# An expert stage with its turns in another order, two turns in plain float32, and gate scatters in the second stage

## The chip, the cores and the metric

One core of one Trainium2 chip runs the kernel. The metric is the device time of one launch in microseconds; the time of a kernel is the median of its runs.

## The reference

Three stages follow each other: attention within clusters, a mixture of eight experts with one expert per token, and a bilinear layer.

```python
def _attn_ref(q, k, v, centroids):            # 2 x 8 heads, 768 rows, 64 wide; 16 centroids
    ...
    mask = q_assign[:, :, :, None] == k_assign[:, :, None, :]
    scores = np.where(mask, scale * np.matmul(q, k.transpose(0, 1, 3, 2)), -1000000000.0)
    ...
    return np.matmul(attn, v)

def _moe_ref(x, expert_emb, tau, w1, w2):     # 1536 tokens of 512; 8 experts, 1024 hidden features
    ...
    expert_idx = np.argmax(logits, axis=1)
    gate_w = probs[np.arange(N), expert_idx]
    for e in range(E):
        mask = expert_idx == e
        h = np.maximum(x[mask] @ w1[e], 0.0)
        out[mask] = gate_w[mask, None] * (h @ w2[e])
    return out

def _moe2_ref(x, w_a, w_b, w_out):            # 512 -> 1536 -> 512
    return ((x @ w_a) * (x @ w_b) @ w_out)
```

The weights `w_a`, `w_b` and `w_out` of the last layer arrive as 64-bit numbers, all else as float32.

## The kernel before

The order of the work on every engine is the order in which the program is written; nothing reorders it. The program runs attention first (to 299.6 us of the trace), then a loop over `G`: 64 steps of the **expert stage** and 72 steps of the **second stage**, which is the bilinear layer.

**Turns.** The expert stage takes the experts in eight turns of eight steps. Turn 0 is expert 0; `ranks` sorts the others by their token counts on the chip and writes the order into `turn_i`, which SyncE and ScalarE read into registers for the addresses of their loads. `WIDTHS` gives the token columns of each turn; before, they fall from 256 to 160 in the order of the turns. `limits` works out which tokens exceed the widths, `further` where each turn's results go, and `rare` is a block for the excess tokens that is jumped over here (at step `GR` = 5, on every engine that has a part in it).

**A step.** `layer1(G)` makes 128 hidden features of a turn into a PSUM tile (`et0`, `et1` in alternation), ScalarE applies the relu, and `layer2(G - 2)` adds the product with `w2` to the turn's results `ys_ps` in the PSUM banks `sc0` to `sc3`. `trans_x` turns the next turn's tokens at step 5 of a turn (6 in turn 0), and `load_xe` loads them on ScalarE's queue.

**Two halves.** To keep float32 precision with the faster `float32r` format, every operand is split into a rounded high half and the rest as a low half. Three products (high by high, low by high, high by low) make one result. Turns 0 to 2 (`e < TWO`) issue them as three matmuls; later turns issue two, of which the first takes both halves of the tokens side by side (columns twice the width) into two PSUM halves that VectorE adds (`both_halves`, L1162) before it makes the low half of the hidden features (L1157).

**Weights.** An expert has 4 chunks of weights, and each chunk 4 parts of 128 rows by 512. `load_raw` (L151) loads two parts (512 KB) into one of `NRAW` = 4 raw buffers, on SyncE's queue; `split_some` makes the high half on ScalarE (L177) and the low half on VectorE or, for one pair in four from turn 3 on, on GpSimd (L178). The split halves lie in `NSLOT` = 9 chunk slots. A limit (`2 * G + lead`, and a ramp until step 22) sets how far the splits run ahead. After the last split, `narrow_a` to `narrow_d` do the same for the 64-bit weights of the second stage, one part in a step: ScalarE (L1015, L1035) and VectorE (L1027, L1028, L1029, L1041).

**Routing tables.** `result_rows` (turn 2) and `gates` (from step 25 on) work out where a token's row lies and its gate. `gates` then issues twelve scatters of 128 pairs into `tab_d` on GpSimd (L909), each followed by a one-element copy from a tile of the current step (L915), and the read of the table into `res` on SyncE (L917). `res` is needed when the second stage stores its first results. `put_rows` writes a turn's results to `ys_d` on SyncE, and `load_x2` reads columns of `ys_d` for the second stage.

**Second stage.** `bil1(I)` makes 128 columns of both products with 24 matmuls, VectorE multiplies them (L1242), and `bil2(I - 2)` multiplies with `w_out` into the banks `sc0` to `sc3`, `pp` and `pv`.

Of the kernel before, what the change touches and what calls it, by code (L numbers as in the profile page):

```python
# [9 lines left out]
F32 = mybir.dt.float32  # L10
F32R = mybir.dt.float32r
# [13 lines left out]
CAP = 256  # L25
WIDTHS = (256, 256, 248, 224, 216, 192, 176, 160)
TWO = 3
NRAW = 4
# [5 lines left out]
PACE = (1,)  # L34
YW = 0
CG0 = 2
# [8 lines left out]
def kernel(  # L45
# [76 lines left out]

    units = [(m, 2) for m in range(0, 4 * NCE, 2)]
    units += [(m, 1 if wide else 2) for m in range(4 * NCE, 4 * NCH, 1 if wide else 2)]
# [10 lines left out]
    def load_raw():  # L135
        u = nraw[0]
        if u == len(units) or (u >= NRAW and sum(units[u - NRAW]) > ndone[0]):
            return
        m, cnt = units[u]
        if 16 <= m < 4 * NCE and m % 16 == 0:  # L140
            if not ranked:
                return
            turn_e[m // 16] = nc.values_load(turn_i[0:1, m // 16:m // 16 + 1], engines=[mybir.EngineType.SP], min_val=1, max_val=NE - 1)
        nraw[0] += 1
        src = streamed(m // 4)[:, m % 4:m % 4 + cnt, :]
        if src.dtype == I64:
            t = rawp.tile([P, cnt, 512, 2], I32, tag="raw", name=f"raw_{u}")
            nc.sync.dma_start(out=t.rearrange("p c f x -> p c (f x)"), in_=src.bitcast(I32))
        else:
            t = rawp.tile([P, cnt, 512], F32, tag="raw", name=f"raw_{u}")  # L150
            nc.sync.dma_start(out=t, in_=src)  # L151
        for j in range(cnt):
            raw[m + j] = t[:, j]
        if cnt == 2:
            raw2[m] = t

    def open_part():
        n, j = divmod(nsplit[0], 4)  # L160
        if j == 0:

            hl[n] = (big if n % NSLOT else left).tile([P, 2, 4, 512], F32R, tag=f"w{n % NSLOT}", name=f"w_{n}")
        w = raw.pop(nsplit[0])
        nsplit[0] += 1
        return w, hl[n][:, 0, j, :], hl[n][:, 1, j, :]

    def split_some(m):

        for _ in range(m // 2):  # L170
            load_raw()
# [138 lines left out]
    def setup_rest():  # L310
# [581 lines left out]

    def gates(hh):

# [63 lines left out]
    def ranks():  # L958
# [4 lines left out]
        nc.vector.tensor_reduce(out=pbase.rearrange("p o e -> p (o e)"), in_=bef, axis=AX.X, op=ALU.add)  # L963
        nc.vector.tensor_tensor(out=at, in0=row(turn_c), in1=col(pbase), op=ALU.is_equal)
        nc.vector.tensor_tensor(out=prod[0:1], in0=at[0:1].rearrange("p e q -> p q e"), in1=turn_c[0:1].to_broadcast([1, NE, NE]), op=ALU.mult)
# [13 lines left out]
    def further():  # L979

        nc.vector.tensor_tensor(out=prod, in0=col(turn_c), in1=row(turn_c), op=ALU.is_gt)
        summed(obase, prod, row(over))
        summed(pbase, bef, row(held))
        nc.vector.tensor_reduce(out=key[:, 0, 0:1], in_=over.rearrange("p o e -> p (o e)"), axis=AX.X, op=ALU.add)
# [70 lines left out]
    def trans_x(key, src):  # L1055

        x = new_x(key)
# [5 lines left out]
        wd = WIDTHS[key]  # L1063
        for u in range(2):
# [71 lines left out]
    def layer1(G):  # L1136
# [4 lines left out]
        wd = WIDTHS[e]  # L1141
        h2 = big.tile([P, 2, CAP], F32R, tag="hh", name=f"hh_{G}", bufs=4)
# [3 lines left out]
        if e < TWO:  # L1146
            mm3(ph[:, 0, :wd], [(ws[j], (x[:, 0, j, :wd], x[:, 1, j, :wd])) for j in range(DC)])
# [15 lines left out]

    ready = []

    def layer2(G):
# [3 lines left out]
        h2 = hs.pop(G)  # L1170
        wd = WIDTHS[e]
        hh, hlo = h2[:, 0, :wd], h2[:, 1, :wd]
        last = f == NF - 1
        if f == 0:
            banks = (2, 3, 0, 1) if e >= TWO else (e % 2 * 2, e % 2 * 2 + 1)
            ys_ps[e] = [ps_s.tile([P, 2, CAP], F32, tag=f"sc{u}", name=f"y_{e}_{u}") for u in banks]
        if e < TWO:
            for i, (s_, m_) in enumerate(((hh, 0), (hh, 1), (hlo, 0))):
                for j in range(DC):
                    nc.tensor.matmul(ys_ps[e][j // 2][:, j % 2, :wd], w[:, m_, ff, j * P:(j + 1) * P], s_,  # L1180
                                     start=(f == 0 and i == 0 and j % 2 == 0), stop=(last and i == 2 and j % 2 == 1))
        else:
# [185 lines left out]
```

## Time and profile before

| what | value |
|---|---|
| median of 3 runs (lowest, highest) | 802.11 us (799.87, 802.85) |
| profiled execution | 805.78 us, its span 803.4 us |
| TensorE matmul busy | 767.8 us, 96% of the span |
| VectorE busy | 494.9 us, 62% |
| ScalarE busy | 402.3 us, 50% |
| GpSimd busy | 128.2 us, 16% |
| first matmul of the expert stage | 299.64 us |
| first matmul of the second stage | 487.10 us |

The shares are means over three stages with different limits. What bounds the expert stage is read from TensorE's idle time and granted clock in stretches of that stage, from what ended each idle time, and from the instructions that the named engine ran just before.

### The profile page before, as it was taken

What the parts mean: (1) busy time and instruction counts of PE and PEld (TensorE: products, weight loads), DVE (VectorE), ACT (ScalarE), POOL (GpSimd) and SP (SyncE); (2) the same over time, 40 slices, a digit from 0 to 9 for tenths busy, and PEclk for the clock granted to TensorE, in tenths of its full rate; (3) what the DMA queues carried; (4) which work ended last, traced back from release to release, by engine and by line L of the source; (5) the groups of instructions that cost most, each with busy time, mean ns of one, the idle gap of its engine ahead of it and who ended that gap; (6) DMA issues with size and microseconds to landing.
All of it is one profiled execution on the core that took longest, in us unless ns stands there. A gap on an engine that the chain in (4) does not pass through costs nothing.

```text
span 803.4 us, 14115 instructions
## 1 busy us (share of the span) xinstructions
PE 767.8 (96%) x5385; PEld 669.4 (83%) x5385; DVE 494.9 (62%) x998; ACT 402.3 (50%) x860; POOL 128.2 (16%) x145
## 2 busy tenths in 40 slices
PE   8899999998999988998999888999999999999996
PEld 5667777776777668997999877999999999999996
DVE  6677676785657666787888799777762322221221
ACT  4556766767666674575676655444432222221211
POOL 5103203043100050012228500000001110000101
PEclk9899999999999999999999989999999999999999
DMA  6228123163121035788779867534401200000000
GB/s 187 52 75 281 40 79 83 56 190 95 44 46 31 32 126 188 237 283 274 254 250 227 219 222 228 156 115 128 132 1 53 78 28 1 2 27 1 27 1 26
DMA packets 48970, 91.95 MB, mean 114 GB/s; under 512 B 6264, under 2 KB 22264, under 8 KB 48896
## 3 DMA queue, kind: packets, MB, share of 16 engines
q1 hardware_dynamic: 44688, 81.01, 33.8%
q0 software_dynamic: 2304, 6.31, 2.1%
q10 hardware_dynamic: 1904, 3.67, 1.3%
q8 instruction: 43, 0.70, 0.4%
q14 instruction: 31, 0.25, 0.1%
HBM read 69.27 MB, written 14.04 MB: 104 GB/s over the span
## 4 chain that ended last, share of the span: by engine, by line
issue 42%; DMA 7%; PE 6%; POOL 2%; DVE 2%; ACT 1%; POOLq 0%; DVEq 0%; ACTq 0%; SPq 0%
DMA raw<-in_moe_w_dram 6%; PE h L1152 2%; PE y L1184 2%; DVE w L178 1%; ACT w L177 1%; POOL out_dram L1280 1%; POOL w L178 1%; PE h L1153 1%; PE y L1185 1%; DMA tab_d<-id_gate,slot_i 1%; PE y L1180 0%; DMA res<-tab_d 0%; PE h L1075 0%; DVE rr L878 0%; POOL tab_d L909 0%
## 5 line engine op out<-in xcount | busy, mean ns | idle before, releaser
L1075 PEld LDWEIGHTS ab<-xT_b,w 128*128 128x128 f32 x1152 | 143.8, 191 | 5.8 <-DVE hf L1162 2.1
L1075 PE MATMUL ab<-xT_b,w 128*128 128x256 f32 x1152 | 145.4, 282 | 1.9 <-DVE hf L1162 1.9
L1242 DVE TENSOR_TENSOR ga<-ab,ga 128x256 f32<-128x256 f32 x72 | 30.5, 424 | 150.3 <-ACT ga L1241 150.3
L533 ACT ACTIVATE E<-sc,nmx 128x768 f32<-128x768 f32 x96 | 86.8, 905 | 58.9 <-DVE nmx L528 47.7
L1241 ACT COPY ga<-ab 128x256 f32<-128x256 f32 x72 | 26.9, 373 | 172.3 <-PE ab L1075 172.3
L1269 PE MATMUL o<-w,g 128*128 128x512 f32 x432 | 111.4, 394 | 1.6 <-DVE ys L1162 1.6
L528 DVE TENSOR_REDUCE nmx<-sc 128x1 f32<-128x768 f32 x96 | 91.4, 953 | 17.9 <-PE sc L520 16.2
L548 PEld LDWEIGHTS et<-ident,E 128*128 128x128 f32 x576 | 64.0, 143 | 37.8 <-ACT ET L552 12.4
L548 PE MATMUL et<-ident,E 128*128 128x128 f32 x576 | 84.2, 283 | 7.0 <-ACT E L533 3.2
L1269 PEld LDWEIGHTS o<-w,g 128*128 128x128 f32 x432 | 76.7, 189 | 14.6 <-DVE ys L1162 1.8
L554 DVE COPY ET<-et 128x384 f32<-128x384 f32 x96 | 52.6, 548 | 57.4 <-PE et L548 57.3
L177 ACT CAST w<-raw 128x1024 fp32r<-128x1024 f32 x64 | 67.4, 1055 | 31.7 <-DMA raw<-in_moe_w_dram 26.4
L178 DVE TENSOR_TENSOR w<-raw,w 128x1024 fp32r<-128x1024 f32 x54 | 65.5, 1217 | 16.6 <-ACT w L177 16.2
L575 PE MATMUL pv<-ET,v 128*64 128x384 f32 (+2 forms) x408 | 74.2, 485 | 0.6 <-ACT ET L552 0.5
L519 PE MATMUL sc<-K,Q 80*128 80x512 f32 x192 | 73.3, 382 | 0.0
L1280 POOL DMA_INDIRECT out_dram<-ot,res x12 | 11.7, 972 | 330.8 <-DVE ot L1279 329.5
L520 PE MATMUL sc<-K,Q 128*128 128x512 f32 x192 | 62.0, 344 | 0.0
L1152 PE MATMUL h<-xT,w 128*128 128x448 f32 (+4 forms) x160 | 51.0, 373 | 4.7 <-DVE hf L1162 2.6
L1184 PE MATMUL y<-hh,w 128*128 128x448 f32 (+4 forms) x160 | 50.9, 373 | 3.5 <-DVE ys L1162 3.5
L1075 PE MATMUL ab<-x2h,w 128*128 128x256 f32 x384 | 53.6, 282 | 0.0
L1075 PEld LDWEIGHTS ab<-x2h,w 128*128 128x128 f32 x384 | 50.8, 191 | 2.0
L1245 ACT CAST g<-ga 128x256 fp32r<-128x256 f32 x72 | 29.3, 406 | 39.1 <-DVE ga L1242 39.1
(254 smaller groups left out, 1349.3 us busy)
## 6 DMA issues: line engine op xcount, KB each, us to landing
raw<-in_moe_w_dram SPq DMA_DIRECT2D x64, 512.0 KB, 5.2
raw<-in_moe_w_a_dram SPq DMA_DIRECT2D x12, 512.0 KB, 3.5
raw<-in_moe_w_b_dram SPq DMA_DIRECT2D x12, 512.0 KB, 3.8
raw<-in_moe_w_out_dram SPq DMA_DIRECT2D x12, 512.0 KB, 3.5
xs_d<-zero SPq DMA_DIRECT2D x8, 512.0 KB, 6.2
xe<-xs_d ACTq DMA_DIRECT2D x7, 512.0 KB, 5.7
v<-in_v_dram SPq DMA_DIRECT2D x8, 384.0 KB, 3.1
K<-K SPq DMA_DIRECT2D x8, 384.0 KB, 3.9
```

Source lines behind the costliest of these rows:

```text
L177: nc.scalar.copy(hi, w)
L178: (nc.gpsimd if n >= 4 * TWO and n % 2 == 0 and j == 0 else nc.vector).tensor_sub(lo, w, hi)
L519: nc.tensor.matmul(ps[:, lo:hi], Q3[:, qs], K3[:, h * S + lo:h * S + hi], start=True, stop=False)
L520: nc.tensor.matmul(ps[:, lo:hi], Q2[:, qs], K2[:, h * S + lo:h * S + hi], start=False, stop=True)
L528: nc.vector.tensor_reduce(out=nmx[pp][:, h, t:t + 1], in_=sc[s], axis=AX.X, op=ALU.max, negate=True)
L533: nc.scalar.activation(e, sc.pop(s), AF.Exp, bias=nmx[pp][:, h, t:t + 1], accum_out=sums[pp][:, t, h:h + 1])
L548: nc.tensor.transpose(pt[:, j * P:(j + 1) * P], e[:, kt * P:(kt + 1) * P], ident)
L575: nc.tensor.matmul(pv[h * D:(h + 1) * D, :], vt[:, h, kt, :], ets[g, h][:, kt, :n * P], start=(kt == 0), stop=(kt == NT - 1))
L1075: nc.tensor.matmul(ps, s_, m_, start=(i == 0), stop=(i == len(ops) - 1))
L1152: nc.tensor.matmul(ph[:, :, :wd], ws[j][0], x[:, :, j, :wd], start=(j == 0), stop=False)
L1184: nc.tensor.matmul(ys_ps[e][j][:, :, :wd], w[:, 0, ff, j * P:(j + 1) * P], h2[:, :, :wd], start=(f == 0), stop=False)
L1269: nc.tensor.matmul(o_ps[ck][t], s_[:, t * P:(t + 1) * P], w_[:, m_], start=(f == 0 and i == 0), stop=(f == NF2 - 1 and j == len(o_f[ck]) - ...
```

## The change

- `WIDTHS` becomes 256, 160, 256, 224, 248, 216, 192, 176: turn 1 is now the narrowest, turn 7 the second narrowest. `RANKS` gives each turn's place in the sorted order, and `further` works out the turn order of the result rows from it (three more instructions on VectorE).
- `KINDS`: turns 0, 2 and 4 issue three matmuls, turns 3, 5 and 6 two, and turns 1 and 7 ("one") a single matmul in plain float32, with no low halves: of their weights, of their tokens and of their hidden features. Their results need two PSUM banks and one copy each on ScalarE and VectorE.
- The weights of turns 1 and 7 are loaded straight into their chunk slots (`load_whole`), past the raw buffers, with no split. The loads of turn 1 stand at steps 3 and 5, those of turn 7 at steps 42, 46 and 50. `skip_whole` lets the splits go on with the next turn.
- All remaining splits have their low half on VectorE.
- `ranks` and `limits` move from ahead of the loop to steps 1 and 2, `further` from step 6 to step 8, and the first `load_xe` from step 1 to 2. `put_rows` writes one step later (`YW`).
- `gates` keeps its arithmetic; its scatters and the read of `res` become `put_gates`, one scatter in each of the second stage's first twelve steps.
- The PSUM banks of a turn's results are taken in the order in which they came free (`y_banks`).

```diff
-WIDTHS = (256, 256, 248, 224, 216, 192, 176, 160)
-TWO = 3
+WIDTHS = (256, 160, 256, 224, 248, 216, 192, 176)
+RANKS = (0, 7, 1, 3, 2, 4, 5, 6)
+KINDS = ["three" if w > 224 else "two" if w > 176 else "one" for w in WIDTHS]
...
-YW = 0
+YW = 1
...
+    wholes = [4 * n + j for n in whole for j in (0, 2)]
+
+    def load_whole(G):
+
+        while wholes and wholes[0] < min(4 * (NSLOT + 2 * (max(G - LAG, 0) // 4)), 2 * G + 40, 4 * NCE if G >= GR else 4 * (NSLOT - 3)):
+            n, j = divmod(wholes.pop(0), 4)
+            if j == 0:
+                if n % 4 == 0:
+                    take_turn(n // 4)
+                slot(n, F32)
+            nc.sync.dma_start(out=hl[n][:, 0, j:j + 2, :], in_=streamed(n)[:, j:j + 2, :])
+
+    def skip_whole():
+        while nsplit[0] // 4 in whole:
+            nsplit[0] += 4
+            ndone[0] += 4
...
-            (nc.gpsimd if n >= 4 * TWO and n % 2 == 0 and j == 0 else nc.vector).tensor_sub(lo, w, hi)
+            nc.vector.tensor_sub(lo, w, hi)
...
+        summed(turn_of, at, row(turn_c))
+        nc.vector.tensor_tensor(out=bef, in0=col(turn_of), in1=row(turn_of), op=ALU.is_gt)
...
-    ranks()
-    limits()
...
+        if kind == "one":
+            for j in range(DC):
+                nc.tensor.matmul(ph[:, 0, :wd], ws[j][0], x[:, 0, j, :wd], start=(j == 0), stop=(j == DC - 1))
+            nc.scalar.activation(hh, ph[:, 0, :wd], AF.Relu)
+        elif kind == "three":
...
-            banks = (2, 3, 0, 1) if e >= TWO else (e % 2 * 2, e % 2 * 2 + 1)
+            y_banks.sort(key=lambda u: y_free[u])
+            take = y_banks[:4 if kind == "two" else 2]
...
+        if G == 1:
+            ranks()
+        if G == 2:
+            limits()
...
         elif I < tot:
             bil1(I)
+            next(pg_, None)
...
+        if 3 <= G < total_f:
+            load_whole(G)
```

Three places show the order on an engine before and now.

VectorE, at the head of the expert stage, before: the end of `limits`, then the first low half of weights (`w`) of the loop and the low half of the hidden features of step 0 (`hh`).

```order
L975 TENSOR_TENSOR held<-cnt,cap 128x8
L976 TENSOR_TENSOR over<-cnt,held 128x8
L977 TENSOR_REDUCE most<-over 1x1
L178 TENSOR_TENSOR w_3518<-raw_2153,w_3518 128x1024
L1149 SCALAR_TENSOR_TENSOR hh_3523<-h_3524,hh_3523 128x256
```

The same place now:

```order
L968 TENSOR_TENSOR cnt<-cnt_p,ebase 128x8
L205 TENSOR_TENSOR w_3515<-raw_2162,w_3515 128x1024
L1192 SCALAR_TENSOR_TENSOR hh_3520<-h_3521,hh_3520 128x256
L205 TENSOR_TENSOR w_3515<-raw_2239,w_3515 128x1024
L994 SCALAR_TENSOR_TENSOR key<-cnt,iota_e 128x8
L995 MEMSET key 128x1
L996 TENSOR_TENSOR bef<-key 128x64
```

Two low halves of weights and the hidden features of step 0 now stand ahead of `ranks` (from `key` on), which came ahead of them.

VectorE in turn 7, one step, before: the sum and low half of the hidden features, then one part of a 64-bit weight (three instructions on `a`, then the low half of the part before it).

```order
L1162 TENSOR_TENSOR hf_7090<-h_7081,hf_7090 128x160
L1157 SCALAR_TENSOR_TENSOR hh_7080<-hf_7090,hh_7080 128x160
L1027 TENSOR_SCALAR a_7076<-a_7076 128x512
L1028 SCALAR_TENSOR_TENSOR a_7076<-raw_6927,a_7076 128x512
L1029 SCALAR_TENSOR_TENSOR a_7076<-raw_6927,a_7076 128x512
L1041 TENSOR_TENSOR w_7021<-a_7022,w_7021 128x512
```

Two steps of turn 7 now:

```order
L1060 TENSOR_SCALAR a_6945<-a_6945 128x512
L1061 SCALAR_TENSOR_TENSOR a_6945<-raw_6822,a_6945 128x512
L1062 SCALAR_TENSOR_TENSOR a_6945<-raw_6822,a_6945 128x512
L1074 TENSOR_TENSOR w_6911<-a_6912,w_6911 128x512
L1060 TENSOR_SCALAR a_6965<-a_6965 128x512
L1061 SCALAR_TENSOR_TENSOR a_6965<-raw_6854,a_6965 128x512
L1062 SCALAR_TENSOR_TENSOR a_6965<-raw_6854,a_6965 128x512
L1074 TENSOR_TENSOR w_6911<-a_6945,w_6911 128x512
```

The two instructions on the hidden features are gone; the weights of the second stage stay.

TensorE in turn 7, before: the end of one `layer2` and the head of the next `layer1`.

```order
L1184 MATMUL y_1_7098<-hh_7116,w_6704 128x2x160
L1185 MATMUL y_1_7098<-hh_7116,w_6704 128x160
L1152 MATMUL h_7218<-xT_6899,w_6783 128x2x160
L1153 MATMUL h_7218<-xT_6899,w_6783 128x160
L1152 MATMUL h_7218<-xT_6899,w_6783 128x2x160
```

One whole step of turn 7 now:

```order
L1187 MATMUL h_6950<-xT_6761,w_6410 128x176 x4
L1230 MATMUL y_0_6923<-hh_6880,w_6545 128x176 x2
L1230 MATMUL y_1_6924<-hh_6880,w_6545 128x176 x2
L1187 MATMUL h_6970<-xT_6761,w_6548 128x176 x4
L1230 MATMUL y_0_6923<-hh_6916,w_6545 128x176 x2
```

A step of turn 1 or 7 has 8 float32 matmuls, where a step of turns 6 and 7 had 16 in pairs.

## Rows read from the trace of the kernel before

**Rows 1.** Windows (from:to us): busy us and instructions per engine, PEclk, DMA share, GB/s.
```profile
299.64:330.00 30.36, 26.37 (x210) 25.43 (x211) 22.11 (x51) 14.50 (x22) 0.00 (x0) 1.00 0.56 182
330.00:365.00 35.00, 34.94 (x294) 34.55 (x294) 27.37 (x40) 22.51 (x33) 2.75 (x1) 1.00 0.89 283
365.00:385.00 20.00, 16.86 (x121) 16.02 (x120) 14.55 (x27) 10.69 (x19) 5.74 (x2) 0.91 0.83 266
445.00:490.00 45.00, 36.98 (x254) 35.54 (x253) 41.02 (x84) 26.05 (x66) 8.24 (x7) 0.92 0.74 220
```

**Rows 2.** Timeline of TensorE: start us, us, instruction, [idle before <-what ended it].
```profile
316.35 1.48 PE L1180 MATMUL y<-hh,w 128*128 128x256 f32 x11 [2.33 <-issue]
...
470.59 0.63 PE L1184 MATMUL y<-hh,w 128*128 128x320 f32 x1 [2.33 <-DVE ys L1162]
...
487.10 3.14 PE L1075 MATMUL ab<-xT_b,w 128*128 128x256 f32 x24 [1.88 <-DVE hf L1162]
...
499.64 1.67 PE L1269 MATMUL o<-w,g 128*128 128x512 f32 x6 [1.59 <-DVE ys L1162]
```

**Rows 3.** Chain that ended last, in order of time: start us, us, what.
```profile
345.01 7.09 DMA raw<-in_moe_w_dram
...
360.84 7.04 DMA raw<-in_moe_w_dram
...
370.24 6.96 DMA raw<-in_moe_w_dram
```

**Rows 4.** Windows as in Rows 1, around the jump over `rare`.
```profile
315.00:320.00 5.00, 3.65 (x32) 3.65 (x32) 1.50 (x2) 0.68 (x3) 0.00 (x0) 1.00 0.35 83
320.00:325.00 5.00, 4.57 (x39) 4.37 (x37) 4.68 (x18) 3.85 (x6) 0.00 (x0) 1.00 0.22 84
```

**Rows 5.** Timeline of VectorE: one step of turn 7, and the head of the loop.
```profile
300.83 0.16 DVE L935 TENSOR_TENSOR cnt<-cnt_p,ebase 128x8 f32<-128x8 f32 x1
...
303.72 1.23 DVE L178 TENSOR_TENSOR w<-raw,w 128x1024 fp32r<-128x1024 f32 x1
...
466.62 0.32 DVE L1162 TENSOR_TENSOR hf<-h,hf 128x160 f32<-128x160 f32 x1
...
467.21 0.42 DVE L1027 TENSOR_SCALAR a<-a 128x512 uint32<-128x512 uint32 x1
...
469.61 0.32 DVE L1162 TENSOR_TENSOR hf<-h,hf 128x160 f32<-128x160 f32 x1
```

**Rows 6.** Timeline of TensorE: steps of widths 256, 176 and 160 where it never idled.
```profile
330.29 1.60 PE L1180 MATMUL y<-hh,w 128*128 128x256 f32 x12
331.73 1.60 PE L1075 MATMUL h<-xT,w 128*128 128x256 f32 x12
...
450.24 0.35 PE L1152 MATMUL h<-xT,w 128*128 128x352 f32 x1
...
452.40 0.35 PE L1152 MATMUL h<-xT,w 128*128 128x352 f32 x1
...
478.26 0.34 PE L1152 MATMUL h<-xT,w 128*128 128x320 f32 x1
...
480.34 0.34 PE L1152 MATMUL h<-xT,w 128*128 128x320 f32 x1
```

**Rows 7.** A plain float32 matmul in attention: its group by form, and its timeline.
```profile
L589 PE MATMUL px<-rmat,xt 128*128 128x144 f32 x96 | 15.3, 294 | 0.0
...
211.36 0.94 PE L589 MATMUL px<-rmat,xt 128*128 128x144 f32 x6
212.05 0.49 PE L519 MATMUL sc<-K,Q 80*128 80x512 f32 x1
```

**Rows 8.** Groups by line: instruction, count | busy us, mean ns of one | idle before.
```profile
L178 DVE TENSOR_TENSOR w<-raw,w 128x1024 fp32r<-128x1024 f32 x54 | 65.5, 1217 | 16.6 <-ACT w L177 16.2
...
L178 POOL TENSOR_TENSOR w<-raw,w 128x1024 fp32r<-128x1024 f32 x10 | 25.3, 2529 | 105.2 <-ACT w L177 98.9 <-DVE xT L1067 6.2
...
L909 POOL DMA_INDIRECT tab_d<-id_gate,slot_i x12 | 13.1, 1094 | 5.3 <-DVE id_gate L905 3.6 <-issue 1.6 <-PE y L1185 0.2
```

More of the change, by code (lines that the diff above doesn't have):

```diff
@@ L121 @@
     NCH = len(chunks)
-    units = [(m, 2) for m in range(0, 4 * NCE, 2)]
+    whole = [n for n in range(NCE) if KINDS[n // 4] == "one"]
+    units = [(m, 2) for m in range(0, 4 * NCE, 2) if m // 4 not in whole]
     units += [(m, 1 if wide else 2) for m in range(4 * NCE, 4 * NCH, 1 if wide else 2)]
@@ L155, in load_raw, with take_turn, slot @@
             raw2[m] = t
+    def take_turn(p):
+        turn_e[p] = nc.values_load(turn_i[0:1, p:p + 1], engines=[mybir.EngineType.SP], min_val=1, max_val=NE - 1)
+    def slot(n, dt=F32R):
+        hl[n] = (big if n % NSLOT else left).tile([P, 2, 4, 512], dt, tag=f"w{n % NSLOT}", name=f"w_{n}")
+    wholes = [4 * n + j for n in whole for j in (0, 2)]
[11 more added lines that the diff above has]
+            ndone[0] += 4
     def open_part():
@@ L161, in open_part @@
         if j == 0:
-            hl[n] = (big if n % NSLOT else left).tile([P, 2, 4, 512], F32R, tag=f"w{n % NSLOT}", name=f"w_{n}")
+            slot(n)
         w = raw.pop(nsplit[0])
@@ L170, in split_some @@
         for _ in range(m // 2):
+            skip_whole()
+            if nsplit[0] >= 4 * NCE:
+                return
             load_raw()
@@ L300 @@
     width_c = left.tile([P, 1, NE], F32, name="width_c")
+    rank_c = left.tile([P, 1, NE], F32, name="rank_c")
     tri = att.tile([P, P], BF16, name="tri", bufs=1)
@@ L963, in ranks @@
         nc.vector.tensor_reduce(out=pbase.rearrange("p o e -> p (o e)"), in_=bef, axis=AX.X, op=ALU.add)
-        nc.vector.tensor_tensor(out=at, in0=row(turn_c), in1=col(pbase), op=ALU.is_equal)
+        nc.vector.tensor_tensor(out=at, in0=row(rank_c), in1=col(pbase), op=ALU.is_equal)
         nc.vector.tensor_tensor(out=prod[0:1], in0=at[0:1].rearrange("p e q -> p q e"), in1=turn_c[0:1].to_broadcast([1, NE, NE]), op=ALU.mult)
@@ L1055, in trans_x @@
     def trans_x(key, src):
-        x = new_x(key)
+        x = new_x(key, F32 if KINDS[key] == "one" else F32R)
         hi, lo = x[:, 0], x[:, 1]
@@ L1063, in trans_x @@
         wd = WIDTHS[key]
+        if KINDS[key] == "one":
+            for u in range(2):
+                (nc.vector.tensor_copy if u else nc.scalar.copy)(hi[:, 2 * u:2 * u + 2, :wd], pts[u][:, :, :wd])
+            xT_t[key] = x
+            return
         for u in range(2):
@@ L1141, in layer1 @@
         wd = WIDTHS[e]
-        h2 = big.tile([P, 2, CAP], F32R, tag="hh", name=f"hh_{G}", bufs=4)
+        kind = KINDS[e]
+        h2 = big.tile([P, 2, CAP], F32 if kind == "one" else F32R, tag="hh", name=f"hh_{G}", bufs=4)
         hh, hlo = h2[:, 0, :wd], h2[:, 1, :wd]
@@ L1174, in layer2 @@
         if f == 0:
-            banks = (2, 3, 0, 1) if e >= TWO else (e % 2 * 2, e % 2 * 2 + 1)
-            ys_ps[e] = [ps_s.tile([P, 2, CAP], F32, tag=f"sc{u}", name=f"y_{e}_{u}") for u in banks]
-        if e < TWO:
-            for i, (s_, m_) in enumerate(((hh, 0), (hh, 1), (hlo, 0))):
+            y_banks.sort(key=lambda u: y_free[u])
+            take = y_banks[:4 if kind == "two" else 2]
+            for i, u in enumerate(take):
+                y_free[u] = 4 * e + 4 + i
+            ys_ps[e] = [ps_s.tile([P, 2, CAP], F32, tag=f"sc{u}", name=f"y_{e}_{u}") for u in take]
+        if kind != "two":
+            ops = ((hh, 0), (hh, 1), (hlo, 0)) if kind == "three" else ((hh, 0),)
+            for i, (s_, m_) in enumerate(ops):
                 for j in range(DC):
                     nc.tensor.matmul(ys_ps[e][j // 2][:, j % 2, :wd], w[:, m_, ff, j * P:(j + 1) * P], s_,
-                                     start=(f == 0 and i == 0 and j % 2 == 0), stop=(last and i == 2 and j % 2 == 1))
+                                     start=(f == 0 and i == 0 and j % 2 == 0), stop=(last and i == len(ops) - 1 and j % 2 == 1))
         else:
@@ L1187, in layer2 @@
             yts = big.tile([P, DC, CAP], F32, tag="xe", name=f"ys_{e}", bufs=2)
-            if e < TWO:
+            if kind != "two":
                 for u in range(2):
```

28 lines of the change are left out of this document (18 added, 10 removed).

## The prediction, made before the changed kernel ran

> **What bounds the kernel now.** I read first the windows of the expert stage for TensorE's idle time and its granted clock, because its 96% over the span is a mean of three stages. There the losses sit in three places [rows 1]. From 299.64 to 330 us TensorE idles 30.36 - 26.37 = 4.0 us. From 330 to 365 it never waits. From 365 to 385 it idles 3.1 us, and the granted clock is 0.91, which takes 20 x 0.09 = 1.8 us more: 4.9 us. From 445 to 490 it idles 8.0 us at a clock of 0.92, another 3.6 us: 11.6 us. Together 20.5 us; the rest of the stage is full.
>
> Next, what ended those waits, from TensorE's timeline [rows 2]. At 316 us it is "issue", right behind the jump over `rare`. In the last stretch it is VectorE: turn 7's first results waited 2.33 us for a PSUM bank (`ys`), and the second stage's first matmul waited 1.88 us for `hf`. The second stage then loses 1.59 us more on `ys`.
>
> Third, why VectorE was late. Around 370 us the chain of waits is a loop: a raw load of about 7 us, cast, subtraction, the next load into the same buffer [rows 3]. Four buffers of 512 KB per 7 us are 300 GB/s, so the loop runs at the speed of the DMA, and the hidden features stand in VectorE's queue behind a subtraction that waits for its load. In turn 7 no load is missing. A step costs VectorE 469.61 - 466.62 = 2.99 us, of which 2.40 is one part of a 64-bit weight and 0.59 the hidden features [rows 5]; TensorE would need 480.34 - 478.26 = 2.08 [rows 6]. VectorE is the bound there, and is 91% busy from 445 to 490 [rows 1].
>
> **The change part by part.**
>
> *Plain float32 in turns 1 and 7.* What goes: a step of width 160 takes 2.08 us and one of 176 takes 452.40 - 450.24 = 2.16 [rows 6], 8 x (2.08 + 2.16) = 33.9 us. What comes: 64 matmuls per turn. The trace has float32 matmuls in attention, `px`: 48 in the program (8 head pairs, 6 blocks) are 96 in the trace, so each runs as two. Six of 144 columns take 212.05 - 211.36 = 0.69 us, 115 ns each or 0.80 ns per column [rows 7]: 1.92 cycles at 2.4 GHz, and I take 2 (0.833 ns). Then 128 x 160 x 0.833 = 17.1 us and 128 x 176 x 0.833 = 18.8 us, together 35.8: **+1.9 us**. The lower bound is `px` as it stands, 34.4 us, +0.5. For the upper I take the overhead of the 176 steps: 2.16 / 8 = 270 ns for a pair of 528 columns, which stream in 220, so 25 ns per matmul; on 256 matmuls that is 6.4 us more, +8.3.
>
> The row shows that six float32 loads of weights and six matmuls fit in 0.69 us, so the loads are hidden [rows 7]. The Trainium skill ("TensorE: Matmul & The Clock Gate", sections LDWEIGHTS and "Weight-path perf modes — Fast Weight Load (FWL) and DoubleRow") says that fast weight load is off for FP32 and that a load of 128 columns takes 128 / 1.2, some 107 ns. By the rule alone 256 loads take 27 us, hidden as long as a matmul (133 to 147 ns by the estimate above) covers each; exposed, the change would lose that. The case in which cover fails is a rival below.
>
> *The work that goes with it.* 16 of 64 casts go from ScalarE. Of the low halves, 54 stood on VectorE (1217 ns) and 10 on GpSimd (2529 ns) [rows 8]; now 48 stand on VectorE, 6 x 1.217 = 7.3 us fewer. Turn 7's hidden features leave VectorE, 8 x 0.59 = 4.7 us, turn 1 never puts any there, and in both the results need one copy instead of four sums. None of this is on TensorE's path by itself; it counts in the places below.
>
> *Head of the loop.* Of the 4.0 us idle, the 2.33 behind the jump stays, as the jump does. `ranks` and `limits` held VectorE from 301.0 to 303.7 [rows 5]; the first low halves now come ahead, so the raw loads behind them go out up to 2.7 us earlier. The other 1.7 us were waits for low halves of turn 1's weights, which no longer exist. I take **-1.0**; between -1.7 and +2, the latter if the fetch behind the jump takes twice as long with more loads in flight.
>
> *365 to 385.* While SyncE jumps, from 315 to 325, the DMA moves 83 and 84 GB/s [rows 4], against 283 afterwards [rows 1]. Eight whole loads of turn 1 (4.2 MB) now stand at steps 3 and 5, four ahead of the jump, and need no buffer and no split. They can use the 10 us x (283 - 84) GB/s = 2.0 MB left idle, 7 us of DMA. Against that, turn 1 lasts 17.1 instead of 8 x 2 x 1.44 = 23.0 us [rows 6], so the steps up to 22, where the ramp asks for three parts a step, come 6 us earlier. The loop of loads is then about as late as TensorE, some 1 us better than before relative to it, and without the wait that brought the clock to 0.91. I take **-3.5** of the 4.9; between -4.9 and +3, the latter if the gap is filled only half.
>
> *445 to 490.* Splits end at step 44, since turn 7 has none, and the 64-bit weights start at step 50, when a chunk slot is free (before, at 53). In steps 50 to 55, width 192 (some 2.3 us, between the 2.16 of 176 and the 2.88 of 256 [rows 6]), VectorE needs 0.6 to 0.75 + 2.40, about 3.1: it falls 0.8 behind in each, 5 us in all. TensorE tolerates about a step, since `et0` and `et1` alternate: about 1 us of waits. Turn 7's first results then meet turn 6's sums in the banks, as the 2.33 us of before: 2.5 us. In turn 7 itself TensorE needs 18.8 / 8 = 2.35 per step, and nothing it waits for comes from VectorE. With 1 us for the clock 4.5 of 11.6 us stay: **-7.1**; between -10 and -3.
>
> *Start of the second stage.* VectorE is some 3 to 5 us behind, where it was behind by as much; the two banks of turn 7 are freed by one copy each. I take **0**; between -1.6 and +2.
>
> *What costs nothing.* The twelve scatters, 13.1 us on GpSimd [rows 8], leave the stage for steps in which GpSimd is idle. The read of `res` waits on SyncE for the last of them at step 12 of the second stage, in front of five raw loads; the four buffers ahead of it hold four steps of work, over 10 us, and `res` is used at step 27. Were that cover gone, one split would be late, 2.4 us on VectorE. `further` and its three instructions (small ones, such as `cnt` with 0.16 us [rows 5]) come two steps later, still before the first results are written. Turn 7's whole loads stand at steps 42, 46 and 50, 14 steps or fewer ahead of use, when the splits' loads have ended. `put_rows` one step later delays no load of step 57 or after.
>
> **The sum.** +1.9 - 1.0 - 3.5 - 7.1 + 0 = -9.7 us. Against the profiled execution, 805.8 us of which 803.4 are span, that is 796.1; against the median of 802.1, **792.4**.
>
> **The rivals.**
>
> *The DMA keeps the pace.* If SyncE's own jump holds back the second four whole loads, the same bytes pass by step 22 at the same time as before, and the 6 us that turn 1 gave are waited for: +2.5 in place of -3.5. VectorE then also enters the tail later, -5. Sum 1.9 - 1.0 + 2.5 - 5 = -1.6: 800.5. For it: 283 GB/s is already near what the loop reached. Against it: four loads are ahead of the jump.
>
> *Everything hidden.* All lower bounds: +0.5 - 1.7 - 4.9 - 10 - 1.6 = -17.7: 784.4. Against it: VectorE's 3.1 us per step in turn 6.
>
> *The float32 matmuls don't overlap with their loads.* Place: turns 1 and 7. A single `px` lasts 294 ns on average [rows 7]; at that spacing 256 take 75.3 us, 41.4 more than before: 802.1 + 41.4 - 11.6 = 832. It makes the kernel slower from 193 ns each: 49.5 us, +15.6, against the -11.6 of the other terms, over +4. Against it stands 115 ns at 144 columns. The skill's rule on fast weight load would work this way.
>
> *Turn 1's weights come late.* Eight whole loads, four raw and two of tokens, 7.3 MB, go out from about 307 us, and the last chunk is needed at step 14, about 339 us: 230 GB/s are enough, and 283 were seen [rows 1]. Each us later is a us of TensorE, and with it the clock: 15 us late would give 809, slower from 14 on.
>
> **How the numbers follow.** Forecast (785 to 798) 0.72; DMA keeps the pace (798 to 804) 0.15; everything hidden 0.05; no overlap 0.04; late weights 0.04. The kernel's measurement can tell about 0.5%, 4 us, from no change. Below 798.1: 0.77; within 4 us: 0.14; above 806.1: 0.09. The range of 8 in 10 takes the forecast's bounds and half of the first rival: 785 to 801.
>
> **What would show each step.** Turn 1 at 17 us and turn 7 at 19 without a wait: the float32 price. Over 200 GB/s from 315 to 325 and no VectorE wait at steps 22 to 25, clock 1.00: the third term. VectorE's steps in turn 7 of 2.40 us, at most 5 us of idle time in turns 6 and 7, and a second stage that starts near 476 us instead of 487: the fourth. Wrong would be a spacing of the float32 matmuls above 160 ns, a wait of turn 1 for its weights, a longer idle time behind the jump, or a second stage slowed by the scatters on GpSimd.

## The result, and the profile after

| what | before | after |
|---|---|---|
| median (lowest, highest) of 4 runs | 800.99 us (796.68, 802.85) | 788.05 us (787.12, 790.61) |
| ratio, 95% interval | | 0.9851 [0.9802, 0.9900] |
| span of the profiled execution | 803.4 us | 785.1 us |
| attention (to the first matmul of the expert stage) | 299.64 us | 296.17 us |
| expert stage (to the first matmul of the second stage) | 187.46 us | 173.72 us |
| start of the second stage | 487.10 us | 469.89 us |

The kernel became 12.9 us faster; 9.7 were forecast, and 788.05 lies in the range. The spans differ by more, 18.3 us: 13.7 in the expert stage, 3.5 in attention and 1.1 in the second stage. The program of attention is the same; it took 295.5 to 300.0 us in the runs below, and its length goes with the granted clock: 0.94, 0.93 and 0.93 from 0, 25 and 175 us for 25 us each before, 1.00 in all three after. That part is not counted as the change's. All below is compared by the length of the expert stage.

Windows of the expert stage after, in the columns of [rows 1] (PE, PEld, DVE, ACT, POOL busy, PEclk, DMA share, GB/s): the whole stage, its head, the two stretches up to 380 us (from 380 to 430 us TensorE never waits), the tail, and the two stretches of [rows 4].

```profile
296.17:469.89 173.72, 168.28 (x1256) 164.88 (x1257) 132.12 (x264) 97.14 (x189) 1.26 (x1) 1.00 0.81 265
296.17:330.00 33.83, 31.24 (x249) 30.67 (x250) 18.18 (x49) 11.79 (x22) 0.00 (x0) 1.00 0.73 252
330.00:360.00 30.00, 29.99 (x241) 29.66 (x239) 22.97 (x36) 19.63 (x30) 0.00 (x0) 1.00 0.87 291
360.00:380.00 20.00, 19.27 (x134) 18.17 (x134) 18.55 (x37) 14.15 (x27) 0.00 (x0) 1.00 0.92 278
430.00:469.89 39.89, 37.78 (x260) 37.20 (x259) 35.63 (x73) 23.38 (x58) 0.00 (x0) 1.00 0.76 250
315.00:320.00 5.00, 5.00 (x45) 5.00 (x44) 1.20 (x3) 1.19 (x3) 0.00 (x0) 1.00 0.68 253
320.00:325.00 5.00, 5.00 (x42) 5.00 (x42) 3.31 (x18) 0.61 (x2) 0.00 (x0) 1.00 0.62 216
```

TensorE idles 173.72 - 168.28 = 5.4 us in the stage and the clock is 1.00; before it idled 187.46 - 172.24 = 15.2 us at a mean clock of 0.97. VectorE's busy time fell from 153.1 to 132.1 us, ScalarE's from 113.4 to 97.1, GpSimd's from 45.7 to 1.3.

TensorE's waits, from its timeline (start us, us, instruction, [idle before <-what ended it]); [rows 2] are the ones of before.

```profile
306.58 1.10 PE L1113 MATMUL h<-xT,w 128*128 128x256 f32 x7 [0.87 <-DVE w L205]
...
309.41 1.67 PE L1113 MATMUL h<-xT,w 128*128 128x256 f32 x12 [0.30 <-PEq L1119]
...
312.62 0.63 PE L1230 MATMUL y<-hh,w 128*128 128x256 f32 x4 [1.42 <-issue]
...
360.73 1.45 PE L1113 MATMUL h<-xT,w 128*128 128x256 f32 x10 [0.64 <-DVE hh L1192]
...
451.34 1.46 PE L1187 MATMUL h<-xT,w 128*128 128x176 f32 x8 [0.46 <-DVE hf L1205]
...
456.78 1.46 PE L1230 MATMUL y<-hh,w 128*128 128x176 f32 x8 [1.65 <-DVE ys L1205]
...
482.08 0.97 PE L1319 MATMUL o<-w,g 128*128 128x512 f32 x3 [0.21 <-DVE ys L1240]
```

These seven waits are all that is left above 0.2 us; the last lies in the second stage. The tail keeps 0.46 + 1.65 = 2.1 us of 11.6, and the second stage starts without a wait for `hf`.

The same timeline in the float32 turns: half steps of turn 1 (160 columns) and of turn 7 (176).

```profile
327.76 1.25 PE L1187 MATMUL h<-xT,w 128*128 128x160 f32 x8
328.84 1.25 PE L1230 MATMUL y<-hh,w 128*128 128x160 f32 x8
329.93 1.25 PE L1187 MATMUL h<-xT,w 128*128 128x160 f32 x8
...
462.86 1.36 PE L1187 MATMUL h<-xT,w 128*128 128x176 f32 x8
464.05 1.36 PE L1230 MATMUL y<-hh,w 128*128 128x176 f32 x8
465.24 1.36 PE L1187 MATMUL h<-xT,w 128*128 128x176 f32 x8
```

Four float32 matmuls of the program are eight here, as `px` was in attention. A step takes 329.93 - 327.76 = 2.17 us and 465.24 - 462.86 = 2.38 us: 136 and 149 ns for each of the 16.

### The profile page after: what moved, and what is told of

The parts are those of the page before. It is cut to its first block, busy times and chain, and to the rows that moved or that the text cites. A ratio compares the mean times of both kernels' runs of the same rounds, so it can differ in the third digit from the quotient of the medians.

```text
span 785.1 us, 13982 instructions
## 1 busy us (share of the span) xinstructions
PE 759.6 (97%) x5385; PEld 664.2 (85%) x5385; DVE 466.9 (59%) x955; ACT 383.5 (49%) x820; POOL 105.8 (13%) x143
## 4 chain that ended last, share of the span: by engine, by line
issue 32%; PE 19%; DVE 5%; DMA 2%; POOL 1%; ACT 1%; SPq 0%; POOLq 0%; ACTq 0%; DVEq 0%
PE ab L1113 4%; PE y L1230 3%; PE h L1195 2%; PE y L1234 2%; PE h L1113 2%; PE o L1319 2%; DMA raw<-in_moe_w_dram 2%; DVE a L1061 1%; PE h L1196 1%; PE y L1235 1%; POOL out_dram L1330 1%; DVE w L1074 1%; DVE w L205 1%; PE h L1187 1%; PE xT L1095 1%
## 5 line engine op out<-in xcount | busy, mean ns | idle before, releaser
L1113 PEld LDWEIGHTS ab<-xT_b,w 128*128 128x128 f32 x1152 | 144.0, 191 | 3.7
L1113 PE MATMUL ab<-xT_b,w 128*128 128x256 f32 x1152 | 145.6, 283 | 0.0
L577 PEld LDWEIGHTS et<-ident,E 128*128 128x128 f32 x576 | 62.4, 141 | 37.5 <-ACT ET L581 12.5
L577 PE MATMUL et<-ident,E 128*128 128x128 f32 x576 | 82.4, 279 | 7.3 <-ACT E L562 3.2
L205 DVE TENSOR_TENSOR w<-raw,w 128x1024 fp32r<-128x1024 f32 x48 | 58.2, 1220 | 17.5 <-ACT w L204 16.9
L1230 PE MATMUL y<-hh,w 128*128 128x256 f32 (+3 forms) x416 | 59.3, 289 | 3.1 <-DVE ys L1205 1.6
L204 ACT CAST w<-raw 128x1024 fp32r<-128x1024 f32 x48 | 50.4, 1051 | 16.3 <-DMA raw<-in_moe_w_dram 11.6
L1230 PEld LDWEIGHTS y<-hh,w 128*128 128x128 f32 x416 | 54.5, 190 | 3.5 <-DVE ys L1205 1.9
L1113 PE MATMUL ab<-x2h,w 128*128 128x256 f32 x384 | 53.6, 282 | 0.0
L1113 PEld LDWEIGHTS ab<-x2h,w 128*128 128x128 f32 x384 | 50.8, 191 | 2.0
L581 ACT COPY ET<-et 128x384 f32<-128x384 f32 x96 | 45.7, 476 | 2.7 <-PE et L577 2.7
```

The lines of the kernel that those rows point to most:

```text
L205: nc.vector.tensor_sub(lo, w, hi)
L577: nc.tensor.transpose(pt[:, j * P:(j + 1) * P], e[:, kt * P:(kt + 1) * P], ident)
L1113: nc.tensor.matmul(ps, s_, m_, start=(i == 0), stop=(i == len(ops) - 1))
```

## The experiments

Every kernel is the changed one with the edit shown. "Stage" is the expert stage of its trace; the ratio is to the kernel before, timed on the same chip.

**The control**, the changed kernel once more: 786.52 us, ratio 0.9829 [0.9795, 0.9863], stage 173.8 us.

> The changed kernel itself, beside the three that follow: expert stage 173 to 175 us, time near 788.

**Float32 in neither turn.**

```diff
-KINDS = ["three" if w > 224 else "two" if w > 176 else "one" for w in WIDTHS]
+KINDS = ["three" if w > 224 else "two" for w in WIDTHS]
```

> The changed kernel with turns 1 and 7 as two matmuls per product, so no turn in plain float32 and no whole loads; new order, moved scatters and ranks stay. The expert stage (first matmul of it to first matmul of the second stage) lasted 187.5 us in the profile before and 173.7 after. Theory: the two float32 turns carry the gain, by taking VectorE's work from turn 7 and turn 1's weights from the loop of raw buffers; without them TensorE's own work is 2.5 us less, but 8 to 11 us of waits on VectorE come back in turns 6 and 7 and some 4 us on raw loads before: stage 183 to 188 us, time 797 to 802. Rival: the order of the turns and the moved small work carry it: stage 174 to 178 us, time 788 to 793.

801.92 us, ratio 1.0008 [0.9978, 1.0039], stage 186.1, as the theory had it. Without the float32 turns nothing is gained, though order, scatters and tables are as in the changed kernel. So the float32 turns carry the gain in this order of turns. The waits divide otherwise than expected, 8.4 us from 320 to 385 us (for some 4) and 5.7 from 440 us on (for 8 to 11). The next two runs ask which of the two turns it is.

**Turn 1 in two matmuls, turn 7 alone in float32.**

```diff
+KINDS[1] = "two"
```

> The changed kernel with only turn 7 in plain float32; turn 1 is split and issues two matmuls. Theory: the tail stays free (waits under 3 us after turn 6), but turn 1's 4.2 MB pass the four raw buffers again, while its narrow steps ask for them faster; the waits on raw loads in turns 1 to 3 come back with 4 to 8 us: stage 177 to 181 us. Rival: the loop of raw loads was no limit once GpSimd's subtractions and scatters are gone: stage 172 to 174 us.

797.59 us, ratio 0.9942 [0.9917, 0.9967], stage 182.3: 8.5 us longer than the control and above the theory's 177 to 181. TensorE's waits around turn 1, then ScalarE and VectorE ahead of the first of them:

```profile
332.92 0.42 PE L1235 MATMUL y<-hh,w 128*128 128x320 f32 x1 [3.65 <-DVE ys L1241]
...
356.76 2.19 PE L1231 MATMUL y<-hh,w 128*128 128x256 f32 x12 [2.77 <-DVE ys L1206]
```

```profile
330.07 1.04 ACT L205 CAST w<-raw 128x1024 fp32r<-128x1024 f32 x1 [2.20 <-DMA raw<-in_moe_w_dram]
```

```profile
329.33 2.34 DVE L206 TENSOR_TENSOR w<-raw,w 128x1024 fp32r<-128x1024 f32 x2
331.60 0.31 DVE L1206 TENSOR_TENSOR hf<-h,hf 128x160 f32<-128x160 f32 x1
331.94 0.33 DVE L1201 SCALAR_TENSOR_TENSOR hh<-hf,hh 128x160 fp32r<-128x160 f32 x1
332.19 0.68 DVE L1241 COPY ys<-y 128x512 f32<-128x512 f32 x1
```

Two things meet here: a raw load is late, and the two-matmul form needs all four banks, so that turn 1 has to wait until VectorE, behind the low halves, has copied turn 0's results. The granted clock then falls to 0.88 and 0.78 (330 to 335, 335 to 340 us). Which of the two matters is the question of the run after the next.

**Turn 7 in two matmuls, turn 1 alone in float32.**

```diff
+KINDS[7] = "two"
```

> The changed kernel with only turn 1 in plain float32; turn 7 (width 176) is split and issues two matmuls. Theory: VectorE's hidden features (0.6 us) and splits meet the 64-bit weights (2.4 us) in turns 6 and 7 against 2.2 us of TensorE per step: 8 to 11 us of waits, less 1.8 us of TensorE's work: stage 180 to 184 us, and VectorE over 95% busy in turn 7. Rival: the tail's gain came from the scatters and GpSimd's subtractions that left: stage 172 to 175 us.

792.38 us, ratio 0.9862 [0.9831, 0.9894], stage 175.4: 1.6 us longer, where 6 and more were expected by the theory that turn 7's float32 carries the tail. Waits from 440 us on are 4.5 us against 2.1, of which the cheaper matmuls give back 8 x (2.38 - 2.16) = 1.8; the granted clock falls to 0.91 and 0.75 (455 to 460, 460 to 465 us), which takes 1.7 back. VectorE is 96% busy from 440 us to the end of the stage, as the theory had it, but that costs TensorE little. The theory's sum fell. The time loses a little more than the stage: in this trace the first 25 us of the second stage ran at a granted clock of 0.93.

**Turn 1 in three matmuls**, with two banks and no sums, but with its splits:

```diff
+KINDS[1] = "three"
```

> The changed kernel, but turn 1 (160 wide) issues three float32r matmuls like the wide turns: two banks, one copy each and no sums, while its weights are loaded in parts and split again. With two matmuls the stage was 182.3 us. Its matmuls take about 24 x 80 ns = 1.9 us a step, 15.4 us instead of 17.4. Theory (what turn 1 gains are the splits: loads past the raw buffers and past VectorE): the loop of raw loads is late again, TensorE waits at least 5 us between 320 and 385 us, stage of 177 to 183 us. Rival (the two-matmul form was the loss: its results need four banks and four sums): hardly a wait, stage of 172 to 175 us.

793.42 us, ratio 0.9903 [0.9872, 0.9934], stage 179.9: in the theory's 177 to 183, but for another reason. TensorE's timeline:

```profile
322.95 1.47 PE L1114 MATMUL h<-xT,w 128*128 128x160 f32 x12
324.26 1.64 PE L1231 MATMUL y<-hh,w 128*128 128x256 f32 x12
325.74 1.47 PE L1114 MATMUL h<-xT,w 128*128 128x160 f32 x12
327.04 1.50 PE L1231 MATMUL y<-hh,w 128*128 128x160 f32 x12
```

Twelve matmuls of 160 columns take 1.30 us, 109 ns each, where I had put 80; eight float32 ones take 1.085. In this form turn 1 is 8 x 2 x (1.30 - 1.085) = 3.4 us longer on TensorE itself. Waits from 320 to 385 us are 3.2 against 1.0 in the control, not the 5 of the theory, and none is for `ys`. So turn 1's splits cost some 2 us of waits, its `ys` waits in the run before came from the four banks, and most of the rest of float32's gain over this form is plain matmul time.

**The whole loads of turn 1 all behind the jump.**

```diff
-        if 3 <= G < total_f:
+        if 6 <= G < total_f:
```

> The changed kernel, but no whole load of turn 1 goes out before step 6, so none stands ahead of SyncE's jump. The changed kernel has an expert stage of 173.8 us and moves 253 and 216 GB/s from 315 to 325 us. Theory (turn 1's gain is that the DMA queue has work during the jump, so that the loop of loads is not late afterwards): the two stretches fall to below 150 GB/s, turn 1 waits 2 to 4 us for its first chunk, the splits behind it are 2 MB, some 7 us of DMA, later, and TensorE waits for VectorE between 340 and 385 us: stage of 178 to 182 us. Rival (turn 1's gain is VectorE's 9.7 us of low halves and the missing sums, and the loads have slack): a wait of at most 2 us at the first chunk and none later, stage of 174 to 176 us.

788.29 us, ratio 0.9836 [0.9798, 0.9874], stage 174.5: 0.7 us longer, in the rival's range. The theory, which is the prediction's reason for its third term, fell. Windows of this kernel (the changed one moves 283, 253, 216 and 365 GB/s in these stretches):

```profile
310.00:315.00 5.00, 3.52 (x29) 3.25 (x28) 1.56 (x2) 1.32 (x2) 0.00 (x0) 1.00 0.56 192
315.00:320.00 5.00, 5.00 (x45) 5.00 (x44) 1.01 (x3) 0.81 (x2) 0.00 (x0) 1.00 0.60 189
320.00:325.00 5.00, 4.58 (x37) 4.37 (x36) 3.58 (x18) 0.69 (x2) 0.00 (x0) 1.00 1.01 370
325.00:330.00 5.00, 5.00 (x41) 5.00 (x40) 0.69 (x1) 1.19 (x3) 0.00 (x0) 1.00 1.02 371
```

Eight whole loads that need no raw buffer run at 370 GB/s and make up for the late start; turn 1 waits 0.42 us in all. So the 283 GB/s of [rows 1] were not the DMA's limit. That they were the pace of four buffers that wait for their split fits, but no run had more buffers.

**The turns in falling order**, the two narrowest in float32 at the end:

```diff
-WIDTHS = (256, 160, 256, 224, 248, 216, 192, 176)
-RANKS = (0, 7, 1, 3, 2, 4, 5, 6)
+WIDTHS = (256, 256, 248, 224, 216, 192, 176, 160)
+RANKS = (0, 1, 2, 3, 4, 5, 6, 7)
```

> The changed kernel with the turns in falling order of width again (256, 256, 248, 224, 216, 192, 176, 160), of which the last two are in plain float32. Theory: the tail is free of waits, as neither turn 6 nor 7 needs VectorE; the loop of raw loads in turns 1 to 3 is as before, with 4 to 6 us of waits and a lower clock: stage 175 to 179 us. Rival: the order does nothing: stage 172 to 174 us.

788.21 us, ratio 0.9818 [0.9793, 0.9844], stage 173.6, the control's within 0.2. The order by itself does nothing as long as two turns are in float32: a wait of 1.74 us at 370.68 comes, and the two in the tail go. Turn 1 is 256 wide here and split as before, yet the waits from 355 to 385 us are 2.8 us at a clock of 1.00, where the kernel before lost 4.9 from 365 to 385 us with its clock. So some of that loss goes without any change to turn 1; which part of the change does it was not tried by itself.

**The scatters back in the expert stage**, at steps 38 to 50:

```diff
-    pg_ = put_gates(lambda: gs_[max(gs_)][0])
+    pg_ = put_gates(lambda: hs[max(hs)][:, 0])
...
-            if G > 3 * NF:
-                next(gg, None)
+            if G > 3 * NF and next(gg, 7) == 7:
+                next(pg_, None)
...
             bil1(I)
-            next(pg_, None)
```

> The changed kernel with the twelve gate scatters in the expert stage again (steps 38 to 50), read of the table behind them. Theory: they load the DMA engines for some 15 us but nothing there waits closely for a load, so the stage grows by 0 to 1.5 us. Rival: their small packets delayed raw loads and through them VectorE: 3 us or more.

791.62 us, ratio 0.9891 [0.9847, 0.9934], stage 177.2: 3.4 us longer, which is the rival. The prediction had looked for their cost on GpSimd; it lies in the DMA queues. Windows of the changed kernel, then of this one, the first from where the scatters begin:

```profile
410.00:435.00 25.00, 25.00 (x175) 24.53 (x173) 15.79 (x32) 13.23 (x33) 0.64 (x1) 1.00 0.94 294
425.00:430.00 5.00, 5.00 (x35) 4.90 (x35) 1.53 (x4) 1.16 (x4) 0.00 (x0) 1.00 1.03 404
430.00:435.00 5.00, 5.00 (x37) 4.92 (x35) 2.23 (x8) 2.64 (x9) 0.00 (x0) 1.00 1.02 375
435.00:440.00 5.00, 5.00 (x37) 5.00 (x36) 4.37 (x11) 3.05 (x8) 0.00 (x0) 1.00 0.20 49
```

```profile
410.00:435.00 25.00, 24.32 (x167) 23.61 (x166) 14.95 (x29) 12.32 (x32) 12.76 (x21) 1.00 0.92 208
425.00:430.00 5.00, 4.32 (x29) 3.96 (x28) 0.63 (x2) 1.07 (x4) 0.78 (x2) 1.00 1.06 287
430.00:435.00 5.00, 5.00 (x35) 4.93 (x35) 2.30 (x8) 1.99 (x9) 3.67 (x7) 1.00 0.97 266
435.00:440.00 5.00, 5.00 (x37) 5.00 (x37) 4.33 (x12) 2.94 (x9) 1.60 (x4) 1.00 1.09 277
```

With the scatters the engines of the DMA are about as busy, 0.92 against 0.94, and move 208 instead of 294 GB/s over 25 us, and the backlog fills the stretch to 440, which was nearly free. (The 404 GB/s contain a load of tokens that goes out later in this kernel. And eleven scatters make the difference: the first runs at 409 us in the changed kernel too.) Its chain of waits has the store of turn 4's results (start us, us, what); ScalarE's timeline and TensorE's show what was held up:

```profile
417.17 10.86 DMA ys_d<-ys
```

```profile
428.66 0.35 ACT L1198 ACTIVATE hh<-h 128x216 fp32r<-128x216 f32 x1 [5.08 <-DMA ys_d<-ys]
...
453.07 0.66 ACT L1048 ACTIVATE a<-raw 128x512 f32<-128x512 f32 x1 [3.90 <-DMA raw<-in_moe_w_b_dram]
```

```profile
429.71 0.45 PE L1195 MATMUL h<-xT,w 128*128 128x384 f32 x1 [0.68 <-DVE hf L1205]
...
454.60 1.46 PE L1187 MATMUL h<-xT,w 128*128 128x176 f32 x8 [2.57 <-DVE hf L1205]
```

The store takes 10.86 us (3.9 to 7.2 in the changed kernel), and the next `load_xe`, which needs its buffer, stands on ScalarE's queue ahead of the relu; that costs TensorE 0.68 us. Later a 64-bit weight is late, and the relu and `hf` stand behind its cast; that costs 2.57 us, most of the 3.4. The read of the table, which this edit moves as well, is not what that weight waited for: SyncE's timeline has the weight's load (442.81) ahead of it.

```profile
442.81 2.57 SPq L150 DMA_DIRECT2D raw<-in_moe_w_b_dram  x2
445.69 0.38 SPq L949 DMA_DIRECT2D res<-tab_d  x1
```

In the second stage the scatters cost nothing: it lasts 315.2 us with them (changed kernel) and 315.3 without (this one).

**Both undone**, scatters in the expert stage (the edit above) and turn 7 in two matmuls:

```diff
+KINDS[7] = "two"
```

> Two parts undone at once: turn 7 takes the two-matmul form (alone: stage 175.4 us, 1.6 over the changed kernel) and the twelve scatters go back into the expert stage (alone: 177.2, 3.4 over it). Theory (both put off the same VectorE by adding up): stage of 178 to 180 us. Rival 1 (each alone was caught by the same step of slack, and without it the tail of the kernel before comes back): 181 us or more, with at least 9 us of waits from 440 us on. Rival 2 (the scatters' cost is hidden where VectorE is late anyway): at most 177.5 us.

798.59 us, ratio 0.9977 [0.9959, 0.9996], stage 182.7: 8.9 us longer, where 1.6 + 3.4 = 5.0 would be the sum. Rival 1 holds. TensorE's waits in its tail (five of 0.61 to 0.64 us and one of 0.42 left out):

```profile
451.68 0.43 PE L1196 MATMUL h<-xT,w 128*128 128x352 f32 x1 [1.51 <-DVE hf L1206]
...
461.57 0.43 PE L1235 MATMUL y<-hh,w 128*128 128x352 f32 x1 [2.34 <-DVE ys L1206]
...
478.28 1.94 PE L1114 MATMUL ab<-xT_b,w 128*128 128x256 f32 x14 [1.82 <-DVE hf L1206]
```

With 9.2 us from 440 us on, the waits of before, [rows 2], have come back, though the clock stays at 1.00. Either of the two parts alone was mostly caught by the slack that the other had left.

**Smaller parts.** One low half of weights in four back on GpSimd, from turn 3 on:

```diff
-            nc.vector.tensor_sub(lo, w, hi)
+            (nc.gpsimd if n >= 12 and n % 2 == 0 and j == 0 else nc.vector).tensor_sub(lo, w, hi)
```

> The changed kernel with one low half in four back on GpSimd in turns 3 to 6 (8 subtractions of about 2.5 us). Theory: raw buffers are held 1.3 us longer and some VectorE instructions run slower beside GpSimd, while VectorE has room there: stage longer by 0 to 2 us. Rival: VectorE was short of time there and gains 10 us of work less: stage shorter by 1 us or more.

787.42 us, ratio 0.9850 [0.9814, 0.9885], stage 174.5, 0.7 longer: no difference in the time. `ranks` and `limits` back ahead of the loop:

```diff
+    ranks()
+    limits()
...
-        if G == 1:
-            ranks()
-        if G == 2:
-            limits()
```

> The changed kernel with ranks and limits ahead of the loop again. Theory: the first low halves come 2.7 us later, and with them the raw loads behind them; TensorE's waits in the first 20 us grow by 1 to 2 us. Rival: those waits hang on the jump alone, and the turn register is ready earlier: no change within 0.5 us.

788.23 us, ratio 0.9844 [0.9808, 0.9881], stage 175.5, 1.7 longer. The size is the theory's, the reason is not: the wait for a low half falls to 0.24 us (0.88 in the control), but the idle time behind the jump is 2.34 us again, against 1.00 in the control, and the granted clock then falls, to 0.66 in a stretch in which the control has 1.00.

```profile
314.49 1.75 PE L1233 MATMUL y<-hh,w 128*128 128x256 f32 x11 [2.34 <-issue]
...
315.00:320.00 5.00, 5.00 (x32) 5.00 (x32) 0.61 (x2) 0.79 (x2) 0.00 (x0) 0.66 0.88 324
```

The idle time of the whole stage grows by only 0.4 us; the clock's 5 x 0.34 = 1.7 us cover the rest. Behind the jump TensorE idles 0.49 to 1.42 us in every trace that has `ranks` inside the loop, and 2.33 and 2.34 in the two that have it ahead. Why it follows where `ranks` stands is open.

**A wide turn in front of turn 7.**

```diff
-WIDTHS = (256, 160, 256, 224, 248, 216, 192, 176)
-RANKS = (0, 7, 1, 3, 2, 4, 5, 6)
+WIDTHS = (256, 160, 256, 224, 216, 192, 248, 176)
+RANKS = (0, 7, 1, 3, 4, 5, 2, 6)
```

> The changed kernel with the 248-wide turn (three matmuls, two banks, no sums) moved from place 4 to place 6, in front of turn 7; the 216- and 192-wide turns come one place earlier. Theory (what is left in the tail, 0.45 and 1.65 us, is VectorE that has to add the four banks of turn 6 beside the 64-bit weights): both waits vanish, stage of 171.5 to 173 us, time 1 to 2 us below the changed kernel. Rival (the middle needs the wide turn in which VectorE has a low load, and the splits of turns 4 and 5 come under steps that are shorter by up to 0.6 us): 1 to 3 us of waits between 380 and 440 us, stage of 174 to 177 us.

784.72 us (782.78 to 788.01), ratio 0.9811 [0.9767, 0.9855], and a stage of 170.3 us, 3.5 below the control and shorter than the theory's 171.5 to 173. Both tail waits are gone, and so is the one of 0.73 at 360 us. Its windows, the whole stage:

```profile
295.66:465.92 170.26, 167.79 (x1257) 164.92 (x1257) 132.79 (x266) 97.51 (x191) 1.20 (x1) 1.00 0.83 270
```

The stage idles 2.5 us in all. It beats the kernel before clearly and the changed one in its trace; by the times alone the intervals overlap.

## Why the prediction was right, and where it was not

The sign, the time and the places were right, the reasons only in part. Term by term, forecast and measured:

| term | forecast | measured |
|---|---|---|
| float32 in place of the narrow turns | +1.9 | +2.5 |
| head | -1.0 | -1.4 |
| 365 to 385 us | -3.5 | -4.2 |
| 445 to 490 us | -7.1 | -9.5 |
| start of the second stage | 0 | -1.4 |
| sum | -9.7 | -14.0 |

Of the measured sum -12.6 us lie in the expert stage, whose trace became 13.7 us shorter; 1.1 us stand in no term. By the medians the gain is 12.9 us.

*Float32.* Right in mechanism and size: 136 and 149 ns stand against 133 and 147. Sixteen of them per step and 8 steps, 17.4 + 19.1 = 36.4 us against 33.9. The rival in which loads are exposed fell. The weight loads of the float32 matmuls (L1187) last 190 ns on average in the trace, those of float32r (L1113) 189, and the matmuls still follow each other at 136. The Trainium skill ("TensorE: Matmul & The Clock Gate", "Weight-path perf modes — Fast Weight Load (FWL) and DoubleRow") has fast weight load off for FP32. Whether it was on for float32r, no row here shows: the loads of both last equally long.

*Head.* The forecast said that the 2.33 us behind the jump stay; they fell to 1.42 here and 1.00 in the control, and are 2.34 with `ranks` ahead of the loop. Of the 1.7 us that were put down to turn 1's low halves two waits of the kernel before, 1.2 us, were that, and they went:

```profile
325.35 0.74 PE L1075 MATMUL h<-xT,w 128*128 128x256 f32 x4 [0.77 <-DVE w L178]
326.48 1.09 PE L1075 MATMUL h<-xT,w 128*128 128x256 f32 x7 [0.40 <-DVE w L178]
```

In return 0.87 us for a low half came. The size agrees for a partly different reason.

*365 to 385.* The size was right, the reason was not, so that the agreement is luck. Loads ahead of the jump are worth 0.7 us (whole loads behind the jump). The step that failed is "the loop runs at the speed of the DMA": a rate that a loop of four buffers reaches was taken for the limit of the DMA, which moves 370 GB/s when loads need no buffer. What helps is that turn 1's loads leave that loop and VectorE's queue, some 2 us of waits by the run with three matmuls; about 2 us more go in the falling order as well, where turn 1 is as before. That float32 needs neither four banks nor sums counts against two matmuls, not against the kernel before, whose turn 1 had three. The rival "the DMA keeps the pace" rested on the same misreading.

*445 to 490.* The term that was mis-sized, by 2.4 us. The waits of turn 6 and of turn 7's first results came as worked out, only smaller (0.46 for 1, 1.65 for 2.5), and the clock did not fall, for which 1 us was taken. The mechanism was half of it. The prediction put the whole term down to VectorE's work in turn 7, and undoing that work alone costs 1.6 us. The step that failed stands under "What costs nothing": the scatters were counted on GpSimd and SyncE and not on the DMA engines that they share with the loads of the same steps. They cost 3.4 us alone, and 182.7 - 175.4 = 7.3 where turn 7 also makes VectorE late. Turn 7's float32 in turn gives 1.6 us where the scatters have moved, and 182.7 - 177.2 = 5.5 where they have not.

*Start of the second stage.* VectorE is further ahead than I took it to be: the wait for `ys` is 0.21 us, and was 1.61 in the run without float32. The sign of being wrong that was named for this stage, scatters that slow it, did not come.

Of the parts that the prediction did not price one by one, the order of the turns is worth nothing here and GpSimd's low halves under 1 us. What the falling order without float32 would give with the scatters moved was not run, so that how the 13.7 us of the stage divide between float32 and the scatters in the order of before stays open.

## What to carry to other kernels

Before a stream's rate is taken for the limit of the DMA, ask how many buffers it has and what frees them; loads without a buffer in the loop show it. Where operands are split to use a faster format, price the narrow tiles in each form with everything that the form needs: at 160 columns a step takes 2.08 us in two matmuls, 2.17 in plain float32 and 2.61 in three, and only float32 needs neither a low half nor a sum. A part that looks free alone, as the scatters do on their own engine, may be hidden by slack that another part leaves, so undo parts in pairs as well.

## What the runs showed of the hardware

A float32r matmul of 160 columns took 109 ns in a row of twelve, one of 256 columns 1.44 / 12 = 120 ns [rows 6]: 0.68 against 0.47 ns per column, so that little is saved by narrowing it. A plain float32 matmul of the program ran as two, 136 ns each at 160 columns, 0.85 ns per column. Three matmuls in the fast format therefore cost more at this width than one in the slow one, 1.30 us against 1.085 for the same product. What sets the 109 ns was not tried. With ten scatters of 128 pairs (1 KB each) beside the bulk loads, the DMA moved 208 instead of 294 GB/s over 25 us, 0.71 of its rate, at about the same busy share.
